# Attention scores in quarters of the TensorE array, and the opening's planner told so

## The chip, the cores and the metric

The kernel runs on one core of a Trainium2 chip. The metric is the device time of one execution in microseconds (us), as a median over runs. The core's engines are TensorE (PE, with its weight loads shown apart as PEld), VectorE (DVE), ScalarE (ACT) and GpSimd (POOL); SyncE (SP) issues the DMAs. Each engine works through its own list of instructions in program order and waits on semaphores for the others. PE writes into PSUM, which DVE and ACT empty.

## What is computed

A decayed causal attention over 4 batches, 8 heads, 576 positions and head size 64, and two gated feed-forward blocks after it. Cut to what matters:

```
scores = q @ k.T / sqrt(64)                       # per batch and head
ret    = scores * Dmat[head]                      # Dmat = gamma ** (i - j) for i >= j, else 0
x      = ret @ v                                  # 2304 tokens x 512
h = x @ w_in;  x = (h * cos(h)) @ w_out           # 512 -> 2048 -> 512
xn = x / rms(x) * rms_g
out = (silu(xn @ w_gate) * (xn @ w_val)) @ w_out2 # 512 -> 1536 -> 512
```

## The kernel before, in words

**The attention** is worked in chunks of 128 positions: per batch four full chunks and one short chunk of 64. Two batches are worked side by side, so the loop in `opening` (line 842 on) runs over ten pairs k = 0 to 9, with the short chunks at k = 4 and k = 9. Within a chunk the masked scores are computed directly; what comes from earlier chunks comes through a running state (sum of decayed key times value). For each chunk there are these steps:

- `scores` (line 338; its matmul is line 347): for each of the four pairs of heads, two matmuls. The contraction is over the head size, 64, so the even head of the pair takes the upper 64 rows of the array and the odd head the lower 64, each over all 128 columns (128 keys), with 128 moving columns (128 queries). The two run in row halves at the same time, and each of the two halves writes to its own PSUM bank. In a short chunk there are 64 keys, and a matmul already takes a quarter of the array.
- `masked` (L353, on DVE): multiplies a bank by the falling factors into SBUF, one bank at a time.
- `from_state` (L365): queries times state, 64 rows by 64 columns, in quarters of the array in the order (0,0), (1,1), (0,1), (1,0), eight matmuls a chunk.
- `sums_kv` (L379) and `values` (L395): column halves, 128 rows by 64 columns. ACT scales keys (`scale_keys`, L324) and copies the state (`copy_state`, L384).
- `result` (L405, on DVE): moves the output bank into `xall` with the gamma factor.

**The first feed-forward block** starts while the attention still runs. Its weights come in 64-bit words and are turned into float by `Block` (lines 163 to 200): ACT L144 and L154, DVE L148 (clamp), L151 (shift), L157 (high words), L160 (add), then ACT L191 and DVE L136 split them in a high and a low part. A unit is one tile of tokens by one weight block: `hidden` (L242 to L244, three matmuls per product) into a PSUM bank, then the gate: ACT L521, DVE L524 (remainder), ACT L527 (sine), DVE L530 (product, which frees the bank), ACT L534, DVE L136; three units later `out_t` multiplies by the output weights. `FIRST = 6` units use the first token tile, with weight blocks 0 to 5; the next 16 use the second tile and begin again at block 0. While the attention is open there are three general banks, named `g`, shared by scores, the late outputs and `hidden`.

**The order of the work** up to unit 21 comes from a planner. `opening` makes a `Task` for every step, with its engine, a guess of its duration, what it comes after, what buffers it takes and gives, a due time (`key`) and, on PE, a mode: "rows", "quarters", "columns" or "whole". `lay_out` (line 823) then picks task by task. A PE task whose mode differs from the last one's is taken to start `SWITCH` = 0.2 us later (0.3 for "whole"). On each engine, of the tasks that could start within `SLACK` = 0.05 us of the earliest, the one with the least due time is taken:

```
            if x.mode and x.mode != mode[0]:
                begin = max(begin, free[x.engine] + SWITCH + (0.1 if x.mode == "whole" else 0.0))
...
                begin, x = min(((b, x) for b, x in found if b <= first + SLACK), key=lambda bx: bx[1].key)
```

The picks give the program order on PE, DVE, ACT and SP. The planner's times only sort the tasks; on the chip every engine starts when its semaphores let it. Loads on SP are chained one behind another (`PLAN`); `keep_x`, which writes the split first tile to DRAM, is the one other SP task. After unit 21 the order is written out by hand, and the second feed-forward block follows.

The functions that the change touches, and what calls them:

Of the kernel before, what the change touches and what calls it, by code (L numbers as in the profile page):

```python
# [30 lines left out]
P = 128  # L31
B, H, S, D = 4, 8, 576, 64
# [55 lines left out]
def body(ctx: ExitStack, tc, xy, xr, w1, w2, rg, gq, gk, mask, out):  # L88
    nc = tc.nc
# [28 lines left out]
    def acc_tile(m):  # L118
        return (psp if m < KC else late["psh"]).tile([P, 512], F32, tag=f"acc{m}", name="acc")

    def ps_tile():
        if "psh" not in late:
            return psa.tile([P, 512], F32, tag="g", bufs=3, name="g")
        taken[0] += 1
        return hidden_tile() if taken[0] % 2 else acc_tile(KC + taken[0] // 2 % 2)
# [151 lines left out]
    def half(a):  # L277
        return slice(a * D, (a + 1) * D)
# [6 lines left out]
    def load(k, side, parts=(None,)):  # L285
        r, c = divmod(k, NCH)
        for part in parts:
            if len(ld.setdefault(k, [])) == side:
                x = wa.tile([P, 4, DM], F32, tag="w", name="x")
                ld[k].append(x)  # L290
            x = ld[k][side]
            if c == NFULL:
                nc.sync.dma_start(x.rearrange("p s m -> p (s m)"), xr[r])
            else:
                cols = slice(None) if part is None else slice(part * 2, part * 2 + 2)
                nc.sync.dma_start(x[:, cols], xy[r, c, side, :, cols])

    def keys_queries(n):
        b, c = chunks[n]
        k, q = b // 2 * NCH + c, b % 2  # L300
        if c < NFULL:
            parts = [ld[k][0][:, 2 * q + s] for s in range(2)]
        else:
            flat = ld[k][0].rearrange("p s m -> p (s m)")
            parts = [flat[:, (2 * q + s) * NPAIR * REST:(2 * q + s + 1) * NPAIR * REST] for s in range(2)]
        return [x.rearrange("p (a i) -> p a i", a=NPAIR) for x in parts]
# [13 lines left out]
    def scale_keys(k):  # L320
        kk, c = ld[k][1][:, 2:], k % NCH
        for h in range(H):
            x = kk[:, :, h * D:(h + 1) * D]
            nc.scalar.activation(x, x, AF.Copy, scale=decays[:, c * H + h:c * H + h + 1])  # L324
# [4 lines left out]
    def keys(w, a):  # L329
        return slice(None) if w == P else half(a)  # L330

    def spare_banks(n):
        b, c = chunks[n]
        return b % 2 and b // 2 * NCH + c < EARLY
# [5 lines left out]
    def scores(n):  # L340
        w = width(chunks[n][1])
        kt, qt = keys_queries(n)
        tiles = [acc_tile(2 + a) if spare_banks(n) else ps_tile() for a in range(2)]
        ps = raw_scores[n] = [tile.rearrange("p (h i) -> p h i", h=NPAIR) for tile in tiles]
        for p in range(NPAIR):
            for hh in range(2):
                nc.tensor.matmul(ps[hh][keys(w, hh), p, :w], kt[half(hh), p, :], qt[half(hh), p, :], start=True, stop=True)

    def masked(n, hh):
        w = width(chunks[n][1])  # L350
        s = sc[n, hh] = ap.tile([P, NPAIR, P], F32, tag=f"s{hh}", bufs=4, name=f"s{hh}")
        r = keys(w, hh)
        nc.vector.tensor_tensor(s[r, :, :w], raw_scores[n][hh][r, :, :w],  # L353
                                falling[hh if w == P else 2 * hh][r, :, :w], op=ALU.mult)

    def from_state(n):
        b, c = chunks[n]
        w, q, k = width(c), b % 2, b // 2 * NCH + c
        _, qt = keys_queries(n)
        if q == 0:  # L360
            begin_outputs(k)
        for j in range(2):
            for a, b in ((0, 0), (1, 1), (0, 1), (1, 0)):
                p, h = place(a, j, b)
                nc.tensor.matmul(outputs[k][a][half(b), q, j, :w], state[half(a), q, p, :], qt[half(a), p, :],  # L365
                                 start=q == 0 and j == 0, stop=False, skip_group_check=True)

    def sums_kv(n):
        b, c = chunks[n]
        q = b % 2  # L370
        vv, kk = tokens_of(n), ld[b // 2 * NCH + c][1][:, 2 + q]
        if c == 0 and q == 0:
            total[0] = psa.tile([P, 2, NPAIR, D], F32, tag="st", name="total")
        for j in range(2):
            for e in range(2):
                for a in range(2):
                    p, h = place(a, j, a ^ e)
                    cs = slice(h * D, (h + 1) * D)
                    nc.tensor.matmul(total[0][half(a), q, p, :], kk[:, cs], vv[:, cs], start=c == 0 and q == 0 and p == 0, stop=True,  # L379
                                     skip_group_check=True)  # L380

    def copy_state(k):
        for p in range(NPAIR):
            nc.scalar.activation(state[:, :, p, :], total[0][:, :, p, :], AF.Copy, scale=factors[:, k % NCH + 1, p:p + 1])  # L384
# [121 lines left out]
    def hidden(t, f):  # L506
        n = TILES[t][1]
        ps = ps_tile()
        proj(part1("in", f), t, ps)
        return ps[:, :n]  # L510
# [361 lines left out]
    def opening():  # L872
# [8 lines left out]
        def fetch(size, run, *take):  # L881
            queue.append(Task("SP", size, run, (), ones(*take), behind=queue[-1] if queue else None))
            return queue[-1]

        for k in PLAN:
            if k == 0:
                start = [fetch(0.0, load_first, "wa"), fetch(1.3, lambda: load(0, 0, range(1, 2)))]
# [12 lines left out]
        for k in range(B // 2 * NCH):  # L900
            b, c = k // NCH * 2, k % NCH
            full = c < NFULL
            pair = [(b + q) * NCH + c for q in range(2)]
            at = lead(k)
            bank = "acc" if k < EARLY else "g"
            places = {n: "more" if spare_banks(n) else "g" for n in pair}
            masks = {}
            for n in pair:
                score = Task("PE", 0.89 if full else 0.45, lambda n=n: scores(n), [start[0] if n == 0 else loads[k][0]], {places[n]: 2},
                             key=at - 2.0, more=0.25, mode="rows")  # L910
                masks[n] = [Task("DVE", 0.6 if full else 0.35, lambda n=n, hh=hh: masked(n, hh), [score, falls[hh if full else 2 * hh]],
                                 ones(f"s{hh}"), ones(places[n]), key=at - 2.0) for hh in range(2)]
            held = {bank: 1 if k < EARLY else 2}
            last = []
            if c > 0:
                for n in pair:
                    last = [Task("PE", 0.45 if full else 0.22, lambda n=n: from_state(n), masks[n] + before + last, held if n == pair[0] else (),
                                 ones("wa") if full and n == pair[1] else (), key=at, more=0.25, mode="quarters")]
                froms[k] = last
            adding = []  # L920
            if full:
                adding = [Task("ACT", 8 * 0.29, lambda k=k: scale_keys(k), [loads[k][1]], key=at - 1.0)]
                for n in pair:
                    adding = [Task("PE", 0.52, lambda n=n: sums_kv(n), before + adding + loads[k], ones("st") if c == 0 and n == pair[0] else (),
                                   key=at + 0.1, more=0.25, mode="columns")]
                before = [Task("ACT", 4 * 0.3, lambda k=k: copy_state(k), adding + last + froms.get(k - 1, []), (),
                               ones("st") if c == NFULL - 1 else (), key=at - 1.0)]
            for n in pair:
                after = masks[n] + last + loads[k] + (adding if n == pair[1] else [])
                give = {"s0": 1, "s1": 1, "wa": 0 if n == pair[0] else 2 if c == 0 else 1}  # L930
                last = [Task("PE", 0.79 if full else 0.42, lambda n=n: values(n), after, held if c == 0 and n == pair[0] else (), give,
                             key=at + 0.2, more=0.25, mode="columns")]
            freed = [{}, {bank: 1}] if k < EARLY else [{bank: 1}] * 2
            done = [Task("DVE", 0.6 if full else 0.35, lambda k=k, a=a: result(k, a), last + [gams], (), freed[a], key=at - 0.5) for a in range(2)]
            for n in pair:
                evacs[n] = done
        Task("ATT", 0.0, close_attention, [x for done in evacs.values() for x in done], (), {"g": 1, "wb": NSLOT_B})
        ready_w = {}
        for k in range(NW1):
            at = unit(first_use[k]) - LEAD  # L940
# [17 lines left out]
        for i in range(MANUAL):  # L958
            s, t, f = STEPS[i]
            at = unit(i)  # L960
            give = {f"x{kc}": 1 for kc in range(KC)} if i in ENDS else {}
            hiddens[i] = Task("PE", 2.72, lambda i=i: first_half(i), [ready_w[f], hiddens.get(i - 1)] + xs_of[s], ones("g"), give,
                              key=at, more=0.25, mode="whole")
# [35 lines left out]
    for i in range(MANUAL, LAST + LAG):  # L999
        early_out = LAG <= i < LAST and (i - LAG in ENDS or i == MANUAL)  # L1000
        if i < LAST:
# [3 lines left out]
            ps = hidden(t, f)  # L1005
# [360 lines left out]
```

## Time and profile before

| what | value |
|---|---|
| median of 3 runs | 869.49 us (868.59 to 870.76) |
| the profiled execution | 869.32 us |
| its span, first to last instruction | 867.5 us |
| mean granted TensorE clock | 0.998 |
| instructions | 13936, of them 5360 matmul records |

The profile is of one execution. Its span leaves out what lies before the first and after the last instruction. Times within it are us from the span's start. A matmul of f32 operands stands in it as two records, so that the 8 matmuls of one chunk's scores show as x16. The ends of matmuls are modelled, so the distance between two starts is the better measure of what a block of matmuls takes.

### The profile page before, as it was taken

The page shows a single profiled execution, that of the slowest core. Times are in us where ns is not written, and L with a number is a line of the kernel's source. Part 1 is how long each engine was busy: PE and PEld are TensorE (multiplying, and loading weights), DVE is VectorE, ACT ScalarE, POOL GpSimd, SP SyncE. Part 2 cuts the span into 40 slices and gives each one's busy share as a digit, 9 for nine tenths or more (in the row PEclk, how much of TensorE's full clock was granted, in tenths as well). Part 3 has the DMA queues.
Part 4 walks back from the last instruction along what each step waited for, and adds up shares of the span by engine and source line. Part 5 has one row for each costly group of instructions (what it writes and reads, how often), then busy time and mean ns, then how long its engine had stood idle before and what let it go on. Part 6 is the DMA issues. An engine that isn't in the chain of part 4 may idle for free.

```text
span 867.5 us, 13936 instructions
## 1 busy us (share of the span) xinstructions
PE 852.7 (98%) x5360; PEld 780.0 (90%) x5360; DVE 655.7 (76%) x998; ACT 487.3 (56%) x885; POOL 65.7 (8%) x77
## 2 busy tenths in 40 slices
PE   6999999999999999999999999999999999999998
PEld 5887788888888889988889999999999999999998
DVE  3899999857879976997875888898565598343594
ACT  5789786457655566675566565554443353333351
POOL 0000000000000000002443544000000000000000
PEclk9999999999999999999999999999999999999999
DMA  8999401044434443334785888998777797877792
GB/s 344 416 417 414 183 17 48 2 133 154 138 110 145 147 146 102 117 122 154 253 286 219 312 317 321 342 315 267 282 254 245 221 299 273 282 252 253 211 313 101
DMA packets 58530, 193.68 MB, mean 223 GB/s; under 512 B 5472, under 2 KB 20960, under 8 KB 49760
## 3 DMA queue, kind: packets, MB, share of 16 engines
q1 hardware_dynamic: 58464, 192.80, 64.1%
q8 instruction: 42, 0.69, 0.3%
q14 instruction: 24, 0.20, 0.1%
HBM read 143.49 MB, written 49.28 MB: 222 GB/s over the span
## 4 chain that ended last, share of the span: by engine, by line
PE 81%; DMA 9%; DVE 8%; ACT 1%; issue 1%; SPq 0%; ACTq 0%; DVEq 0%
PE h L1104 15%; PE acc L1104 14%; PE acc L243 10%; PE acc L244 10%; PE acc L242 10%; PE acc L1151 10%; DMA x<-xy_dram 6%; PE h L243 3%; PE h L244 3%; PE h L242 3%; DVE SV L1140 3%; DVE w L136 2%; DMA kept_x<-xhi 2%; DMA rg_sb<-rg_dram 1%; ACT w L1132 0%
## 5 line engine op out<-in xcount | busy, mean ns | idle before, releaser
L1104 PE MATMUL acc<-w 128*128 128x384 f32 x720 | 139.3, 335 | 0.2
L1104 PE MATMUL h<-w 128*128 128x384 f32 x720 | 138.8, 335 | 0.5 <-DVE SV L1086 0.5
L1104 PEld LDWEIGHTS h<-w 128*128 128x128 f32 x720 | 125.9, 188 | 1.5 <-DVE SV L1086 0.8
L1104 PEld LDWEIGHTS acc<-w 128*128 128x128 f32 x720 | 126.0, 188 | 0.9 <-DVE v L1092 0.8
L243 PE MATMUL acc<-glo,w 128*128 128x512 f32 (+1 forms) x320 | 117.9, 368 | 0.0
L242 PE MATMUL acc<-ghi,w 128*128 128x512 f32 (+1 forms) x320 | 117.9, 368 | 0.0
L244 PE MATMUL acc<-ghi,w 128*128 128x512 f32 (+1 forms) x320 | 117.7, 368 | 0.0
L1151 PE MATMUL acc<-w 128*128 128x384 f32 x564 | 100.8, 335 | 1.0 <-DVE w L136 1.0
L658 POOL TENSOR_TENSOR z<-z 128x256 f32<-128x256 f32 x72 | 65.3, 909 | 477.8 <-DMA z<-w 416.9
L1151 PEld LDWEIGHTS acc<-w 128*128 128x128 f32 x564 | 98.0, 188 | 1.6 <-DVE w L136 1.6
L1092 DVE TENSOR_TENSOR v<-s,acc 128x384 f32<-128x384 f32 x54 | 29.9, 553 | 52.9 <-PE acc L1104 41.6
L243 PEld LDWEIGHTS acc<-glo,w 128*128 128x128 f32 x320 | 60.3, 188 | 10.5 <-DVE glo L136 0.4
L242 PEld LDWEIGHTS acc<-ghi,w 128*128 128x128 f32 x320 | 60.3, 189 | 10.1
L244 PEld LDWEIGHTS acc<-ghi,w 128*128 128x128 f32 x320 | 60.4, 189 | 9.8
L1132 ACT CAST w<-SV 128x768 fp32r<-128x768 f32 x55 | 42.5, 832 | 33.5 <-DVE SV L1140 18.5
L527 ACT ACTIVATE r<-r,half_pi 128x512 f32<-128x512 f32 (+1 forms) x80 | 54.7, 684 | 11.3 <-DVE r L524 10.8
L1086 DVE TENSOR_TENSOR SV<-s,h 128x384 f32<-128x384 f32 x54 | 29.8, 552 | 41.2 <-PE h L1104 35.6
L534 ACT CAST ghi<-r 128x512 fp32r<-128x512 f32 (+1 forms) x80 | 46.2, 577 | 20.8 <-DVE r L530 20.7
L1070 ACT COPY s<-h 128x384 f32<-128x384 f32 x54 | 25.8, 478 | 55.8 <-PE h L1104 54.4
L136 DVE TENSOR_TENSOR glo<-r,ghi 128x512 fp32r<-128x512 f32 (+1 forms) x80 | 52.2, 653 | 4.2 <-ACT ghi L534 3.2
L136 DVE TENSOR_TENSOR w<-SV,w 128x768 fp32r<-128x768 f32 x55 | 50.5, 962 | 5.6 <-ACT w L1132 5.6
L242 PE MATMUL h<-xhi,w 128*128 128x512 f32 (+1 forms) x148 | 54.2, 366 | 0.0
(130 smaller groups left out, 1596.8 us busy)
## 6 DMA issues: line engine op xcount, KB each, us to landing
w<-so SPq DMA_DIRECT2D x42, 768.0 KB, 5.6
w<-s SPq DMA_DIRECT2D x24, 1024.0 KB, 5.0
raw<-w_dram SPq DMA_DIRECT2D x36, 512.0 KB, 4.0
w<-s SPq DMA_DIRECT2D x24, 768.0 KB, 4.3
raw<-w_dram SPq DMA_DIRECT2D x16, 1024.0 KB, 15.0
x<-xy_dram SPq DMA_DIRECT2D x14, 1024.0 KB, 19.9
s<-w SPq DMA_DIRECT2D x12, 1024.0 KB, 6.2
w<-t SPq DMA_DIRECT2D x36, 256.0 KB, 2.3
```

The lines of the kernel that those rows point to most:

```text
L136: eng.tensor_tensor(dst, src, hi.bitcast(F32), op=ALU.subtract)
L242: nc.tensor.matmul(dst, a[0], b[0], start=start, stop=False)
L243: nc.tensor.matmul(dst, a[0], b[1], start=False, stop=False)
L244: nc.tensor.matmul(dst, a[1], b[0], start=False, stop=stop)
L527: nc.scalar.activation(s["r"], s["r"], AF.Sin, bias=half_pi, scale=1.0)
L534: nc.scalar.copy(s["hi"], s["r"])
L658: nc.gpsimd.tensor_tensor(z[:, dst], z[:, a], z[:, b], op=op)
L1086: nc.vector.tensor_tensor(dst, s, bank, op=ALU.add)
L1092: nc.vector.tensor_tensor(t, s, bank, op=ALU.add)
L1104: nc.tensor.matmul(bank, w[:, wp, kc * P:(kc + 1) * P], x[:, kc], start=k in (0, 1, 3) and kc == 0 and m == 0, stop=kc == 1 and m == 2, sk ...
L1132: nc.scalar.copy(t[:, 0], src)
L1151: nc.tensor.matmul(pair[d][:, :HALF], wi[:, a], s[:, b, i % 2], start=start and i == 0 and p == 0, stop=i == NPR - 1 and p == 2, skip_grou ...
```

## The change

In a full chunk each score matmul of 64 rows by 128 keys is cut in two of 64 rows by 64 keys. The four matmuls of a pair of heads take the four quarters of the array, in the order (0,0), (1,1), (0,1), (1,0), where the first number is the head's row half and the second the half of the keys; they write the same places of the same two banks. Short chunks keep their two matmuls per pair, written out so that they compute what they did. The planner's mode for a score task becomes "quarters", also for the short chunks; the task's guessed duration and due time stay.

```diff
         for p in range(NPAIR):
-            for hh in range(2):
-                nc.tensor.matmul(ps[hh][keys(w, hh), p, :w], kt[half(hh), p, :], qt[half(hh), p, :], start=True, stop=True)
+            for hh, m in ((0, 0), (1, 1), (0, 1), (1, 0)) if w == P else ((0, 0), (1, 1)):
+                nc.tensor.matmul(ps[hh][half(m), p, :w], kt[half(hh), p, m * D:(m + 1) * D] if w == P else kt[half(hh), p, :],
+                                 qt[half(hh), p, :], start=True, stop=True)
...
                 score = Task("PE", 0.89 if full else 0.45, lambda n=n: scores(n), [start[0] if n == 0 else loads[k][0]], {places[n]: 2},
-                             key=at - 2.0, more=0.25, mode="rows")
+                             key=at - 2.0, more=0.25, mode="quarters")
```

## Rows read from the trace of the kernel before

**Rows 1.** The page: busy time, share of the span, instructions of each engine.
```profile
PE 852.7 (98%) x5360; PEld 780.0 (90%) x5360; DVE 655.7 (76%) x998; ACT 487.3 (56%) x885; POOL 65.7 (8%) x77
```

**Rows 2.** Busy us by stretch: start:end, length, engines (instructions), clock, DMA share, GB/s.
```profile
19.40:31.45 12.05, 12.04 (x224) 11.45 (x226) 6.35 (x10) 7.37 (x25) 0.00 (x0) 0.87 1.01 419
31.45:41.00 9.55, 9.10 (x229) 8.08 (x225) 9.32 (x14) 5.61 (x13) 0.00 (x0) 1.00 1.01 411
41.00:69.00 28.00, 27.99 (x420) 23.57 (x420) 27.90 (x43) 25.34 (x58) 0.00 (x0) 1.00 1.01 415
69.00:99.50 30.50, 28.56 (x261) 22.39 (x256) 30.21 (x42) 26.00 (x36) 0.00 (x0) 1.00 0.65 264
...
110.00:440.00 330.00, 330.00 (x1637) 280.76 (x1636) 275.46 (x460) 207.39 (x355) 18.38 (x20) 1.00 0.39 121
```

**Rows 3.** Waits, 30 to 100 us: who <- whom: us in total, times, longest.
```profile
DVE xall L405 <- PE po L395: 2.1, 1, 2.1
PE g L242 <- DVE r L530: 2.0, 4, 0.8
...
PE po L365 <- DVE xall L405: 0.4, 2, 0.2
```

**Rows 4.** Timeline of PE, 15 to 30 us: start, us, line, out<-in, shapes, records.
```profile
15.34 1.10 PE L365 MATMUL po<-x,state 64*64 64x128 f32 x32
19.41 2.08 PE L347 MATMUL g<-x 64*128 64x128 f32 x16 [2.97 <-DMA x<-xy_dram]
21.29 1.66 PE L347 MATMUL acc<-x 64*128 64x128 f32 x16
22.87 1.15 PE L379 MATMUL total<-x 128*64 128x64 f32 x32
...
25.70 1.16 PE L347 MATMUL g<-x 64*128 64x128 f32 x16
...
27.69 1.10 PE L365 MATMUL po<-x,state 64*64 64x128 f32 x32
28.72 1.15 PE L379 MATMUL total<-x 128*64 128x64 f32 x32
```

**Rows 5.** Timeline of PE, blocks of one chunk alone, with what follows each.
```profile
46.39 1.10 PE L365 MATMUL po<-x,state 64*64 64x128 f32 x16
...
48.51 0.67 PE L365 MATMUL po<-x,state 64*64 64x128 f32 x16
49.10 1.97 PE L395 MATMUL po<-s,x 128*64 128x128 f32 x32
...
60.10 1.16 PE L347 MATMUL g<-x 64*128 64x128 f32 x16
61.19 0.50 PE L242 MATMUL g<-xhi,w 128*128 128x512 f32 x1
```

**Rows 6.** Timeline of DVE: the wait at 31.45, weight block 6, the last product.
```profile
31.45 1.29 DVE L405 TENSOR_TENSOR xall<-po,gam 128x512 f32<-128x512 f32 x2 [2.07 <-PE po L395]
...
87.92 0.69 DVE L148 TENSOR_SCALAR t<-t 128x1024 f32<-128x1024 f32 x1
...
91.77 0.68 DVE L151 TENSOR_SCALAR t<-t 128x1024 int32<-128x1024 int32 x1
...
93.88 1.22 DVE L157 SCALAR_TENSOR_TENSOR t<-raw,t 128x1024 int32<-128x1024 int32 x1
95.13 1.23 DVE L160 CUSTOM_DVE_ANT_0 t<-raw,t 128x2048 uint16<-128x2048 uint16 x1
...
98.79 0.69 DVE L530 TENSOR_TENSOR r<-g,r 128x512 f32<-128x512 f32 x1
```

**Rows 7.** Timeline of PE, 99 us: the first matmul of unit 6, its idle time before.
```profile
99.53 0.51 PE L242 MATMUL g<-xhi,w 128*128 128x512 f32 x1 [0.77 <-DVE r L530]
```

**Rows 8.** Busy us by stretch around the load that lands at 19.41, columns as in Rows 2.
```profile
19.00:21.00 2.00, 1.58 (x14) 1.59 (x16) 0.00 (x0) 0.00 (x0) 0.00 (x0) 0.53 1.00 414
...
23.00:26.00 3.00, 3.00 (x68) 2.83 (x70) 1.66 (x3) 2.34 (x9) 0.00 (x0) 1.00 1.00 410
```

## The prediction

> **What bounds the kernel now.** I read the busy line of the page first. The reader is to see that TensorE (PE) is busy in 98% of the span [rows 1]: time falls only where PE loses work or an idle gap. The scores belong to the opening, so next I cut that into stretches. From 19.40 to 31.45 PE is busy 12.04 of 12.05 us while VectorE (DVE) works 6.35. From 41 to 69 both are full (27.99 and 27.90 of 28.00). From 69 to 99.5 DVE is full (30.21 of 30.50) and PE has 1.94 us of gaps; from 110 to 440 PE has none [rows 2]. The waits name the gaps: four times the projection (L242) waits for the product L530, which frees its PSUM bank, 2.0 us together, and twice `from_state` waits for an evacuation, 0.4 us. DVE for its part has one wait worth a row between 30 and 100 us, 2.1 us for the `values` matmuls of L395; it ends at 31.45 [rows 3, 6]. So the chain changes hands: a load that lands at 19.41, PE until 31.45, DVE's list until 99.53, where PE begins unit 6 [rows 4, 6, 7], then PE to the end. What PE saves before 31.45 brings DVE's list forward; what it saves between 31.45 and 99.5 mostly makes the L530 gaps longer; and by then all scores are done.
>
> **The matmuls.** There are 16 full chunks (k = 0 to 3 and 5 to 8, two batches each); the four short chunks already use quarters and keep their two matmuls per head pair, so only their planner mode changes. A full chunk goes from 8 matmuls to 16. The trace records each f32 matmul twice, so its 16 records become 32, and PE's count becomes 5360 + 16 x 16 = 5616.
>
> In row halves two chunks take 25.70 to 27.69 = 1.99 us [rows 4] and one alone takes 60.10 to 61.19 = 1.09 [rows 5]: a chunk is worth 0.90 and the change of array mode 0.19. The kernel's own quarter matmuls, `from_state` at L365 with 64x64 weights and 128 moving columns, show the other price: two chunks in 27.69 to 28.72 = 1.03 [rows 4], one alone in 48.51 to 49.10 = 0.59 [rows 5], so 0.44 per 8 matmuls and 0.15 for the mode. Twice 0.44 is 0.88 against 0.90. The same work runs twice as often, each piece on half the columns, four pieces at a time instead of two. I take 0.88: the same shapes in the same order of quarters. The upper bound is 1.80, if the two quarters of one row half did not overlap; unlike L365 they read the same moving rows at once, and no row shows that. Weight loads are hidden beside the matmuls in both forms. So the matmuls alone give 16 x 0.02 = 0.3 us on PE, of which four chunks (k = 2 and 3, between 19.41 and 27.69) lie on the chain: 4 x 0.02 = 0.1 us.
>
> **The mode change.** Between a score block and a neighbouring `from_state` block the array now stays in quarters. That removes 0.15 to 0.19 us per border. Three such borders show: at 15.34, where PE afterwards waits for the load until 19.41 [rows 4], so it is worth nothing; at 27.69, on the chain, worth 0.17 (the middle); and at 46.39, in the stretch where DVE is full [rows 2, 5], worth nothing. The Trainium skill (TensorEngine Tiling (Array Packing), Tiling Modes, Key Properties) says that changing the tiling mode, not just the tile, drains TensorE. It names no time; the 0.15 to 0.19 us agree with it.
>
> **The planner.** Telling it "quarters" takes its 0.2 us off the start of a score task behind `from_state` and the reverse. It picks the next task by start, and by due time within 0.05 us, so tasks change places: on PE a `from_state` may now come between two score tasks; on DVE and ScalarE the masks and state copies that follow them move against weight splitting and the gate's products. SP's loads stay in their chained order, though `keep_x` may be issued past another raw load; it doesn't wait there for the score. POOL has no planned task. In each score block the first mask still waits for nearly the whole block, since a bank's last quarter is the last or last but one matmul. So the masks are no earlier, and they queue behind whatever DVE is doing. The order's effect isn't in the trace of before; I bound it. Gain: the DVE steps that PE doesn't need by 99.53 are four of weight block 6 (L148, L151, L157, L160; first used six units later): 0.69 + 0.68 + 1.22 + 1.23 = 3.8 us [rows 6]. But PE can gain no more than its gaps, 2.0 + 0.4 = 2.4 us [rows 3]. Loss: another such set of four, 3.8 us, ahead of the last product. The likeliest is near zero, since the old order already fills PE and DVE to 99% from 41 to 69: I take 0.
>
> **Sum.** 0.1 + 0.17 is 0.3 us. DVE starts its continuous run at about 31.15 and PE unit 6 at about 99.2. Against the profiled execution that is 869.32 - 0.3 = 869.0; that execution has 1.8 us outside its span of 867.5 and lies 0.17 us under the median, so against the median 869.49 it is **869.2 us**.
>
> **Rivals.** A measurement of this kernel can tell about 0.3%, 2.6 us, from no change: faster means under 866.9, slower over 872.1.
>
> *The new order fills the gaps (faster).* Block 6's steps go behind the last product, and PE runs through from 31.45. For it: 3.8 us of steps could wait. Against: PE must lose all of its 2.4 us of gaps to get to 869.2 - 2.4 = 866.8, barely past the bound. The clock could help: PE idles from 16.4 to 19.41 and then runs at a granted 0.53 (its 1.2 GHz level), and is back at 1.00 (2.4 GHz) in 23 to 26 [rows 8]; the two blocks of 19.41 took 22.87 - 19.41 = 3.46 us instead of 1.99 [rows 4], 1.5 us that a run without the fall would not pay. But nothing in the change shortens the wait for the load, so I expect it again.
>
> *The new order puts work ahead of the last product (slower).* PE begins unit 6 when the L530 of 98.79 frees the bank [rows 6, 7]; DVE has no slack there, so every step planned in front moves it. Four more steps cost 3.8 us: 869.2 + 3.8 = 873.0. It decides for slower from 2.9 us of added steps on. For it: one task list, sorted anew. Against: the due times of weight block 7 lie later than the product's, and only a start earlier by over 0.05 us overrides them.
>
> *The added matmuls cost a start of their own (slower).* If a chunk takes e more, the four on the chain give 4e, and the eight of k = 5 to 8 give 8e less the 2.4 us of gaps. At the upper bound e = 0.90 that is 3.6 + 4.8 = 8.4 us, 877.6; from e = 0.44 on (12e - 2.4 = 2.9) it is over the bound. L365's 0.44 for 16 records speaks against any e. The Trainium skill (TensorEngine Tiling (Array Packing), Instruction Overhead) gives each matmul about 60 cycles on trn2 and advises against taking the tiling factor from a dimension that is already small: an estimate of 25 ns at 2.4 GHz, 0.4 us for 16 more records, which would make 869.2 + 1.6 + 0.8 = 871.6. The 0.44 us for 16 quarter records, 27 ns apart, include any such overhead.
>
> *Nothing moves.* If the planner's order stays and DVE hides the 0.3 us too, it is 869.5, the same verdict.
>
> **The numbers.** The forecast with "nothing moves" has 0.72, the filled gaps 0.13, the steps ahead of the product 0.11, the added starts 0.04: faster 0.13, same 0.72, slower 0.15. The range reaches down past 866.8 to 866.4, since gaps and clock could come together in part, and up to the bound of slower, 872.2; it leaves out the two slower cases, 0.15, and little of the faster one.
>
> **What would show it.** Right: 32 score records per chunk about 27 ns apart, two chunks in about 1.9 us; the DVE evacuation of 31.45 some 0.3 us earlier; the same four product gaps of about 2 us; unit 6 at 99 to 99.5. Wrong: score chunks over 1.3 us; DVE idle between masks after 31; unit 6 before 97 or after 102; more weight steps ahead of the last L530; PE gaps after 110.

## The result: slower, and the profile after

The changed kernel takes 873.36 us (median of 11 runs) against 869.79 us for the kernel before in the same comparison: a ratio of 1.0051, 95% interval 1.0038 to 1.0063. That is slower by more than the 0.3% that counts, and outside the predicted range of 866.4 to 872.2. The profiled execution took 874.0 us, 4.7 us more than that of before; its span is 872.2 us.

First the page of the changed kernel: the busy line, and the lines on its DMA queues.

```profile
PE 852.0 (98%) x5616; PEld 779.2 (89%) x5616; DVE 656.1 (75%) x998; ACT 487.8 (56%) x885; POOL 64.8 (7%) x77
...
q1 hardware_dynamic: 58464, 192.80, 63.8%
q8 instruction: 44, 0.72, 0.3%
```

The 5616 records are as predicted, and PE is busy for 0.7 us less than before [rows 1]. So PE has no more work; it has more idle time. The last line looks harmless, and it is where the time went: 44 packets of an instruction queue, 0.72 MB, which is 16 KB each. PE has 2 x 5616 = 11232 weight loads and matmuls, and 11232 / 44 is about 255 instructions per packet. The page of before has 42 packets there, two fewer for its 512 fewer instructions:

```profile
q8 instruction: 42, 0.69, 0.3%
```

The stretches of the changed kernel, in the columns of [rows 2]:

```profile
19.40:31.45 12.05, 10.27 (x280) 9.37 (x274) 6.24 (x10) 7.30 (x25) 0.00 (x0) 1.00 1.01 414
31.45:41.00 9.55, 7.72 (x214) 7.08 (x211) 9.12 (x14) 5.54 (x13) 0.00 (x0) 1.00 1.01 414
41.00:69.00 28.00, 24.88 (x491) 21.49 (x491) 23.48 (x36) 21.45 (x54) 0.00 (x0) 0.94 1.01 416
```

PE is idle for 1.8 us in the first, 1.8 in the second and 3.1 in the third, where it had 0, 0.4 and 0. DVE, full from 41 to 69 before (27.90 of 28.00), now does 23.48 there. It waits for PE's `values` blocks, as at 31.45 before, but more often, and once for a score block. Its waits from 41 to 69 us, where before it has none (who, for whom, us in total, times, longest):

```profile
DVE xall L406 <- PE po L396: 3.2, 2, 2.5
DVE s L354 <- PE acc L347: 1.1, 1, 1.1
```

All waits from 0 to 115 us, in the same form:

```profile
DVE xall L406 <- PE po L396: 8.4, 4, 3.8
...
PE po L366 <- issue: 2.4, 2, 1.4
PE po L396 <- issue: 2.2, 1, 2.2
...
PE total L380 <- issue: 1.7, 1, 1.7
...
PE acc L347 <- issue: 1.3, 1, 1.3
```

"Issue" is a wait for nothing that the profile shows: the semaphores were there and the engine did not go on. Before, PE's matmuls have no such wait from 30 to 100 us. The timeline of PE shows where these fall; the last number of a row is its count of matmul records:

```profile
26.84 0.80 PE L380 MATMUL total<-x 128*64 128x64 f32 x18
29.33 0.62 PE L380 MATMUL total<-x 128*64 128x64 f32 x14 [1.70 <-issue]
29.74 1.97 PE L396 MATMUL po<-s,x 128*64 128x128 f32 x32
31.49 1.15 PE L380 MATMUL total<-x 128*64 128x64 f32 x32
32.57 1.29 PE L366 MATMUL po<-x,state 64*64 64x128 f32 x29
33.60 0.27 PE L347 MATMUL g<-x 64*64 64x64 f32 x2
33.69 0.28 PE L366 MATMUL po<-x,state 64*64 64x128 f32 x3
33.71 0.53 PE L347 MATMUL g<-x 64*64 64x64 f32 x11
34.08 0.22 PE L347 MATMUL acc<-x 64*64 64x64 f32 x1
34.08 0.22 PE L347 MATMUL g<-x 64*64 64x64 f32 x1
34.14 0.22 PE L347 MATMUL acc<-x 64*64 64x64 f32 x1
34.14 0.28 PE L347 MATMUL g<-x 64*64 64x64 f32 x2
35.74 0.67 PE L347 MATMUL acc<-x 64*64 64x64 f32 x14 [1.32 <-issue]
```

The gap at 29.33 is in the middle of a block of one kind, and so is the one at 35.74: nothing in the program is special there. But from one to the next there are 14 + 32 + 32 + 29 + 2 + 3 + 11 + 1 + 1 + 1 + 2 = 128 records, each with its weight load: 256 instructions. The next two gaps, at 41.92 and 47.99, come after 127 and 128 records more. I call these places marks. Setting the marks against the packets of the instruction queue (from the trace's DMA records, in us from the span's start) gives the table below. "Reaches" and "goes on" are the starts of the matmul records before and behind a mark, and the last column counts from "goes on":

```
              PE reaches  goes on  gap    the block's fetch   next fetch starts after
before   3      34.13      34.37   0.24     31.81-32.83          3.66
before   4      40.36      40.52   0.16     38.03-39.05          3.59
before   5      47.23      47.42   0.20     44.11-45.18          3.08
changed  1      15.73      16.97   1.24     14.36-15.36          3.62
changed  2      22.80      23.15   0.36     20.59-21.61          3.61
changed  3      27.42      29.33   1.92     26.76-27.84          3.82
changed  4      34.20      35.74   1.54     33.15-34.29          3.61
changed  5      40.27      41.92   1.65     39.35-40.41          3.64
changed  6      45.51      47.98   2.47     45.57-46.67          3.77
changed  7      54.01      54.20   0.20     51.75-52.85          3.58
```

At each mark of the changed kernel PE goes on 1.3 to 1.6 us after the block's 16 KB have moved. The next fetch starts 3.6 to 3.8 us after PE goes on, and a packet takes 1.0 to 1.1 us. So while PE starves, one block of 256 instructions costs 3.7 + 1.05 + 1.45 = 6.2 us, however fast PE works. Between its marks 3, 4, 5 and 6 PE needed only 4.87, 4.53 and 3.59 us. The kernel before crosses the same places with at most 0.24 us lost. At its marks 3 and 4 it too goes on 1.5 us after the block has moved: it was already at the edge, and its spare was spent by 16 more records per chunk. At its mark 5 the block has been there for 2.24 us; the 0.20 us there is the step from L365 to L379, a change of array mode.

### The profile page after: what moved, and what is told of

Read it like the earlier page. It is cut to its first block, busy times and chain, and to the rows that moved or that the text cites. A ratio compares the mean times of both kernels' runs of the same rounds, so it can differ in the third digit from the quotient of the medians.

```text
span 872.2 us, 14455 instructions
## 1 busy us (share of the span) xinstructions
PE 852.0 (98%) x5616; PEld 779.2 (89%) x5616; DVE 656.1 (75%) x998; ACT 487.8 (56%) x885; POOL 64.8 (7%) x77
## 4 chain that ended last, share of the span: by engine, by line
PE 84%; DVE 9%; DMA 3%; issue 2%; ACT 1%; SPq 1%; POOL 0%; DVEq 0%; ACTq 0%; POOLq 0%
PE acc L1105 15%; PE h L1105 15%; PE acc L243 10%; PE acc L242 10%; PE acc L244 10%; PE acc L1152 10%; PE h L242 3%; PE h L244 3%; PE h L243 3%; DVE SV L1141 3%; DVE w L136 3%; DMA kept_x<-xhi 2%; DMA x<-xy_dram 2%; PE po L396 1%; PE total L380 1%
```

## The experiments

Theory 1: PE's instruction stream runs dry. Its rivals: theory 2, the planner's new order, and theory 3, something in the score quarters themselves. Each run is compared with the kernel before on the same chip.

**Quarter matmuls, old plan** (the changed kernel with one word put back):

```diff
-                             key=at - 2.0, more=0.25, mode="quarters")
+                             key=at - 2.0, more=0.25, mode="rows")
```

> Quarter matmuls with the planner's mode left at rows, so that PE, DVE and ACT work in the order of before. Theory 1 (PE's instruction stream runs dry: it comes in blocks of 16 KB, 256 instructions, and a chunk of quarter scores has 64 of them where row halves have 32): slower by 3 to 5 us, as the changed kernel; gaps of 1.2 to 2.5 us without a releaser before every 128th matmul record between 16 and 50 us, 6 to 10 us together. Theory 2 (the planner's new order makes it slower): within 1 us of before, and no such gaps.

Measured: 873.36 us against 869.00, ratio 1.0048 (1.0034 to 1.0062). PE's waits in its timeline:

```profile
16.72 0.66 PE L366 MATMUL po<-x,state 64*64 64x128 f32 x13 [0.90 <-issue]
36.75 0.68 PE L347 MATMUL acc<-x 64*64 64x64 f32 x14 [1.04 <-issue]
42.94 0.40 PE L366 MATMUL po<-x,state 64*64 64x64 f32 x12 [1.44 <-issue]
49.00 1.96 PE L396 MATMUL po<-s,x 128*64 128x128 f32 x15 [2.20 <-issue]
```

With the order of before on PE, DVE and ACT the loss is all there, and so are the gaps (5.6 us in these rows; fewer than expected, since at the second and third mark little is lost). The order is not needed for it.

Part of the loss goes with PE's clock, which falls to its lower level after some of PE's idle times (in the changed kernel it is granted at 0.57 from 48 to 52 us, behind the gap at 47.99). The three executions of this run with a granted clock of 0.998 took 871.88 to 872.62 us, against 867.74 to 869.87 for the kernel before at the same 0.998: some 3 us at the same clock. The other three, at 0.994 to 0.996, took 874.10 to 874.18.

**Row-half matmuls, new plan** (the kernel before with the other word):

```diff
-                             key=at - 2.0, more=0.25, mode="rows")
+                             key=at - 2.0, more=0.25, mode="quarters")
```

> Row-half matmuls with the planner's mode at quarters: the changed kernel's order with the old matmuls. Theory 1 (instruction stream): within 1 us of before, gaps without a releaser under 0.5 us each. Theory 2 (order): slower by 3 to 5 us.

Measured: 868.91 us against 869.00, ratio 1.0002 (0.9992 to 1.0012). No matmul waits for "issue" here; a weight load does for 0.6 us at most. The waits from 12 to 104 us:

```profile
PEld g L347 <- issue: 1.4, 6, 0.4
PEld po L365 <- issue: 1.0, 2, 0.6
```

Theory 2 falls. The new order does change PE's gaps before the projection (0.8 us in two, where before had 2.0 in four [rows 3]), but the time stays.

**Quarters in k = 0 to 3 alone, and in k = 5 to 8 alone**, both with the old plan; in `scores`:

```diff
+            k = chunks[n][0] // 2 * NCH + chunks[n][1]
+            if w == P and not (k < 4):        # the other run: k > 4
+                for hh in range(2):
+                    nc.tensor.matmul(ps[hh][:, p, :w], kt[half(hh), p, :], qt[half(hh), p, :], start=True, stop=True)
+                continue
```

The lines of the change follow, for the other chunks.

> Quarters in the eight full chunks of k = 0 to 3 alone, planner's mode rows: 256 more PE instructions before about 27 us, one block. Theory 1: about half of the loss, 1.5 to 3 us; the first gaps without a releaser stand as in the changed kernel up to 36 us (about 5 us together), smaller after. Theory 2: within 1 us of before.

> Quarters in the eight full chunks of k = 5 to 8 alone, planner's mode rows. Theory 1: gaps only after 36 us, where before already crosses its blocks with 0.2 us to spare or less: 1 to 2.5 us slower. Theory 2: within 1 us of before.

Measured: 869.79 us for the first four, ratio 1.0010 (1.0001 to 1.0018), and 872.71 us for the last four, 1.0036 (1.0023 to 1.0049). The first four cost less than the 1.5 to 3 us expected, and the last four, 3.7 us, more than the 1 to 2.5. The first have gaps (1.07 at 17.02, 1.05 at 37.01, 0.77 at 43.24), but the one at 17.02 lies ahead of a load that PE waits for anyway, and after 43 it catches up with the edge. The last four have one large gap, 2.21 us at 48.12, and most of the loss. I read this as: what a gap costs depends on who waits behind it, and at 48 us that is DVE, full there in the kernel before. The clock has a part too: behind that gap it is granted at 0.66 from 48 to 52 us. And the last four spread widely: two of their 12 executions, both with a granted clock of 1.000, took 868.92 and 869.15 us, hardly more than the kernel before, and the other ten, at 0.994 to 0.998, took 871.0 to 874.6. Only one of the twelve has a trace, so whether those two had the gap at 48 us stays open.

**The number of instructions without the quarters.** The kernel before, with every `values` matmul of a full chunk cut in two over its queries:

```diff
-                nc.tensor.matmul(outputs[k][a][half(b), q, j, :w], vv[keys(w, a), h * D:(h + 1) * D], sc[n, a][keys(w, a), p, :w],
-                                 start=c == 0 and q == 0 and j == 0, stop=True, skip_group_check=True)
+                for i in range(0, w, 64):
+                    nc.tensor.matmul(outputs[k][a][half(b), q, j, i:i + 64], vv[keys(w, a), h * D:(h + 1) * D], sc[n, a][keys(w, a), p, i:i + 64],
+                                     start=c == 0 and q == 0 and j == 0 and i == 0, stop=True, skip_group_check=True)
```

> The kernel before, scores in row halves and its order unchanged, but every values matmul of a full chunk is cut in two over its 128 queries: 16 records more per chunk, as many as the change adds to the scores, with the same columns streamed in all. Theory 1 (number of PE instructions): slower by 3 to 5 us, with gaps of 1 to 2.5 us without a releaser before every 128th matmul record between 16 and 50 us. Theory 3 (something about the score quarters themselves, such as their weight loads): within 1.5 us of before and no such gaps.

Measured: 876.28 us against 869.29, ratio 1.0081 (1.0062 to 1.0099). Its PE waits:

```profile
31.24 0.51 PE L396 MATMUL po<-s,x 128*64 128x64 f32 x11 [0.34 <-issue]
37.26 1.62 PE L396 MATMUL po<-s,x 128*64 128x64 f32 x46 [1.45 <-issue]
43.67 0.46 PE L396 MATMUL po<-s,x 64*64 64x64 f32 x15 [1.92 <-issue]
50.24 1.16 PE L347 MATMUL acc<-x 64*128 64x128 f32 x15 [1.72 <-issue]
57.46 0.73 PE L396 MATMUL po<-s,x 128*64 128x64 f32 x16 [2.18 <-issue]
```

The scores are in row halves, the order is that of before, and the gaps come all the same, 6.0 to 7.2 us apart. Theory 3 falls: it is the count. It costs more than the 3 to 5 us expected, and more than the change. Two things can add to it, and no run separates them. Four of its gaps, 1.4 to 2.2 us, stand between 37 and 57 us, on the path to DVE. And the cut matmuls aren't quite free by themselves: a `values` block of two chunks takes 2.02 us here (46.13 to 48.15), where before has 1.85 (43.45 to 45.30).

**Why is a fetch so slow?** Theory A: its packet queues behind the loads, which keep the DMA engines full (a share of 1.01 in the stretches above). Theory B: it takes that long in any case. A first pair thinned the weight loads to 1 KB of 8 per partition, with zeros from GpSimd in the rest, once in the kernel before and once in the changed one:

```diff
-            eng.dma_start(self.raw.rearrange("p n c w -> p (n c w)"), src.bitcast(I32))
+            flat = self.raw.rearrange("p n c w -> p (n c w)")
+            nc.gpsimd.memset(flat[:, 256:].bitcast(F32), 0.0)
+            eng.dma_start(flat[:, :256], src.bitcast(I32)[:, :256])
```

> The kernel before, but each load of a block of the first weights moves 1 KB of its 8 KB per partition, and GpSimd fills the rest with zeros, so that the product with most of these weights is left out. It is the pair's other half to the next run: after the attention's own loads are in, the DMA engines are no longer full. Both theories: no gap without a releaser over 0.5 us; time within 3 us of before, since VectorE's work is unchanged.

> The changed kernel with the same thin weight loads and the same part left out. Theory A (a block of PE instructions is late because its fetch queues behind the loads on full DMA engines): where the engines are not full, the 3.6 to 3.8 us between crossing a mark and the start of the fetch shrink below 2.5 us, the gaps without a releaser after 40 us go, and the run is within 1.5 us of the thin row halves. Theory B (the fetch takes as long however busy the engines are): 3.6 to 3.8 us everywhere PE is starved, gaps of 1.2 to 2.5 us as in the changed kernel, 3 to 5 us slower than the thin row halves.

Measured: 873.86 us for row halves, ratio 1.0050 (1.0033 to 1.0068), and 878.99 us for quarters, 1.0105 (1.0086 to 1.0124). The gaps stayed (2.48 us at 47.80), and the difference of 5.1 us is what theory B expected or a little more. But the pair does not decide, since the loads that were left kept the engines full until about 54 us, past the gaps, and there theory A expects the same. The row halves also missed their own expectation of 3 us, which is told in the last section. So a second pair thinned the attention's loads of k = 5 to 8 to a quarter as well:

```diff
+                if k > NFULL:
+                    nc.gpsimd.memset(x[:, 1:], 0.0)
+                    cols = slice(0, 1)
                 nc.sync.dma_start(x[:, cols], xy[r, c, side, :, cols])
```

> As the thin row halves, and in addition every attention load of k = 5 to 8 moves one quarter of its bytes, with zeros in the rest: those chunks are left out of the result, but their instructions all run. The loads should be done by about 40 us, so that the DMA engines are idle while PE still works on k = 5 to 8. Both theories: no gap without a releaser over 0.5 us.

> The same in the changed kernel, with the same parts left out. Theory A (the fetch of a block of PE instructions queues behind the loads): gaps without a releaser as before at the first four marks, up to about 36 us, while the engines are full; then the wait from a mark to the start of the next fetch falls from 3.6 to 3.8 us to under 2.5 us, and the gaps of 1.6 and 2.5 us that stand at 40 to 48 us in the changed kernel shrink to under 0.5 us. Time within 2.5 us of the run with few loads in row halves. Theory B (the fetch takes as long however busy the engines are): the gaps at 40 to 48 us stay at 1.2 to 2.5 us with 3.6 to 3.8 us to the start of each fetch; slower than its row halves by 3 to 5 us.

Measured: 873.19 us for row halves, ratio 1.0053 (1.0034 to 1.0073), and 874.31 us for quarters, 1.0069 (1.0051 to 1.0087). The difference of quarters to row halves is 1.1 us, where it was 5.1 in the pair before. Two stretches of the quarters with few loads, in the columns of [rows 2], and its PE waits from 12 to 60 us:

```profile
40.00:44.00 4.00, 3.40 (x130) 2.99 (x132) 4.00 (x8) 4.00 (x12) 2.48 (x2) 1.00 0.57 222
44.00:48.00 4.00, 3.89 (x84) 3.12 (x82) 4.00 (x8) 4.00 (x14) 1.59 (x1) 1.00 0.92 304
```

```profile
16.48 0.66 PE L371 MATMUL po<-x,state 64*64 64x128 f32 x13 [0.80 <-issue]
29.35 0.62 PE L385 MATMUL total<-x 128*64 128x64 f32 x14 [0.56 <-issue]
34.66 0.67 PE L352 MATMUL acc<-x 64*64 64x64 f32 x14 [0.23 <-issue]
```

The same two stretches of the changed kernel:

```profile
40.00:44.00 4.00, 2.56 (x115) 2.31 (x109) 3.24 (x6) 3.98 (x11) 0.00 (x0) 1.00 1.01 414
44.00:48.00 4.00, 1.80 (x47) 1.56 (x43) 2.63 (x5) 3.09 (x12) 0.00 (x0) 1.00 1.00 410
```

With the DMA share at 0.57 and 0.92 instead of 1.00, PE's gaps for instructions are gone and DVE is full, though the zero fills may be slowing it too (last section). The marks of the run with few loads:

```
              PE reaches  goes on  gap    the block's fetch   next fetch starts after
quarters 1      15.42      16.48   1.07     13.99-14.97          3.59
quarters 3      28.57      29.35   0.78     26.90-27.97          2.72
quarters 4      34.21      34.66   0.44     32.07-33.21          1.21
quarters 5      40.36      40.36   0.00     35.86-36.79          1.45
quarters 6      44.64      44.65   0.00     41.81-42.82          1.56
quarters 7      49.80      49.80   0.00     46.21-47.35          0.53
```

Marks 5 to 7, without a gap, prove nothing by their last column. Where nothing starves PE, a fetch can begin earlier than the array shows: in the kernel before, the fetch that comes in order behind the mark at 174.28 starts at 169.45. And with full engines the kernel before crosses a mark freely at 56.09 and has its next fetch 0.95 us later. What can be compared are marks at which PE starved. After every gap over 1 us in the runs with full engines the next fetch starts about 3.5 us later or more. At mark 4 here PE starved too (it goes on 1.45 us after its block has moved), and the next fetch starts after 1.21 us. The stretches from going on to that fetch, in the columns of [rows 2], at mark 4 of the changed kernel, at mark 4 of this run, and at 56.09 of the kernel before:

```profile
35.74:39.35 3.61, 3.61 (x86) 3.37 (x90) 3.33 (x6) 0.83 (x1) 0.00 (x0) 1.00 1.05 431
34.66:35.86 1.20, 1.20 (x25) 1.13 (x26) 1.20 (x2) 0.33 (x2) 1.20 (x1) 1.00 0.44 145
56.09:57.04 0.95, 0.95 (x32) 0.78 (x30) 0.95 (x2) 0.95 (x2) 0.00 (x0) 1.00 1.04 431
```

The first two are the same place in the same list of instructions, with a DMA share of 1.05 and of 0.44. So 3.6 us is not a fixed delay, which is theory B. Nor does the fetch wait until PE has come to a fixed place in its block, a rival not listed above: PE was 86 records past the mark in one and 25 in the other. The transfer itself stays at about 1.0 us, and the gaps at the early marks, expected as in the changed kernel, are smaller too. Theory A holds in this: how late the fetch of a block of PE instructions starts depends on the loads. One starved mark shows it directly, and the gaps that go agree. Where the fetch waits, in a queue of the DMA engines or ahead of it, no run shows.

No run points to a version that beats the kernel before: the quarters win nothing that shows once they are fed (1.1 us slower with few loads, where DVE is full), and before loses at most 0.6 us at its listed marks.

## Why the prediction was wrong

**The step that failed** is the part on the matmuls. It counted 256 more records, priced them by PE's time alone, 0.88 us a chunk, and put the instructions that carry them at nothing, without a reason. In its place the runs show that a block of 256 instructions costs 6.2 us while the DMA engines are full, and PE gaps of 8.1 us at marks 2 to 7 above. The price it took was right: in the changed kernel two chunks of scores take 24.06 to 25.86 = 1.80 us with no mode change behind them.

```profile
24.06 1.10 PE L347 MATMUL g<-x 64*64 64x128 f32 x32
24.99 1.05 PE L347 MATMUL acc<-x 64*64 64x128 f32 x32
25.86 1.05 PE L366 MATMUL po<-x,state 64*64 64x128 f32 x32
```

That is 0.19 us less than the 1.99 of [rows 4]; the prediction had 0.21, 0.17 for the mode and 0.04 for the matmuls. But blocks of 16 and 32 records, which it read the price from, are shorter than a block of 128, so they cannot show what a steady stream costs. What could have been read before: the page's 42 packets of the instruction queue, 16 KB or 256 instructions each; the small "issue" waits in front of weight loads; and, at marks 3 and 4, that PE goes on just 1.5 us after its block has moved, where mark 5 has 2.24. The distance of the packets, 6.1 to 6.4 us from 25 to 50 us, could not by itself tell a floor from PE's own pace. But it would have made a late block of instructions a rival with a price.

**The chain** was read rightly, and it says how the gaps become time. DVE's list waits for PE's `values` blocks: the evacuation that started at 31.45 starts at 31.53 instead of the predicted 31.15, after a wait of 3.82 us, and it waits 2.46 us once more at 49.09. Between 41 and 69 us DVE waits 4.3 us where before it had no wait. Unit 6 begins at 103.93 instead of 99.53 [rows 7], 4.4 us late, and the span ends 4.7 us late:

```profile
31.53 1.29 DVE L406 TENSOR_TENSOR xall<-po,gam 128x512 f32<-128x512 f32 x2 [3.82 <-PE po L396]
...
49.09 1.29 DVE L406 TENSOR_TENSOR xall<-po,gam 128x512 f32<-128x512 f32 x2 [2.46 <-PE po L396]
```

```profile
103.93 0.50 PE L242 MATMUL g<-xhi,w 128*128 128x512 f32 x1 [0.18 <-DVE r L531]
```

The gaps at marks 2 to 7 are 8.1 us where the listed marks of before have 0.6. Not all of that arrives. In this execution the load for k = 2 let PE start at 18.92 instead of 19.41, and its clock did not fall there (1.00 from 19 to 21), so that its first two blocks took 1.91 us instead of 3.46 [rows 4, 8]: 2.0 us back. I don't count it to the change: the run with the new plan alone waits longer for that load, 3.31 us, and keeps a clock of 1.00 there as well. After the gap at 48 us the clock fell instead: in the stretch from 48 to 52 it is granted at 0.57, and the score block of 49.41 took 1.76 us, where that of 24.06 took 0.93. The prediction had the clock as a possible gain alone.

Of its own signs of being wrong two came, DVE idle after 31 us and unit 6 after 102. The score chunks stayed under 1.3 us, as it held.

**The planner** was put at 0 with bounds of 2.4 us of gain and 3.8 of loss: right, since the new order alone measures 1.0002. The mode change fits in size: with the matmuls' 0.04 it makes 0.21 us, and 0.19 came.

**The rivals.** Steps put ahead of the last product: not so, since the new order alone costs nothing; that its 873.0 lies next to the measured 873.36 is luck. The added matmuls cost a start of their own: the sign was right and the cause not. That rival had the same e for every chunk, and L365's 27 ns per record was rightly held against it; the loss is not per matmul but per 256 instructions, and only where the fetch is slow. So its chance of 0.04 was too small, as it was the one case in which more instructions cost anything at all.

The Trainium skill (Runtime: NRT & Kernel Launch, Instruction fetch mechanics) says that an engine's instructions are refilled in blocks of 16 KiB, 256 instructions, by a DMA queue of the sequencer's own, and that crossing a boundary is mostly hidden. The traces agree on the block: 16 KB packets, and gaps 128 records apart. They disagree on the hiding where the DMA engines are full and PE's matmuls are small: 1.2 to 2.5 us at five of the seven marks of the changed kernel. Here the measurement decides.

## What to carry to other kernels

Count PE's instructions, not only its time: a matmul cut in pieces of the same total streaming time is free only while the stream of 256-instruction blocks keeps pace. Compare the time PE takes for 128 f32 matmul records with the time in which a block of instructions came here while loads kept the DMA engines full, 6.2 us; where PE needs less, every added instruction is on the path. The distance between packets alone says nothing: from 170 to 230 us of the kernel before they are 28 to 30 us apart because PE takes that long for 256 instructions of larger matmuls, and none of its marks there is late. A wait for "issue" in the middle of a block of one kind, repeated at a fixed count of instructions, is the sign, and the first thing to ask is what keeps the fetch waiting.

## What was not expected of the hardware

- One late block of instructions costs PE up to 2.5 us, and how late its fetch starts depends on the other traffic: 3.5 us or more after a starved mark with the DMA engines full, 1.2 us after one at a share of 0.44.
- The fetch is only one block ahead while PE starves: at marks 2 to 7 of the changed kernel a block's packet starts after PE went on at the mark before it.
- GpSimd's zero fills slowed DVE in the runs with thin loads. L151 of DVE takes 0.69 us by itself; beside a fill it took 2.04, and over the seven of the first 100 us its mean rose from 689 to 1076 ns, that of L148 from 683 to 834. That is 3.8 us on a full DVE and would account for most of the 4.6 us that the thin row halves lost; no run has the thin loads without the fills. From the timelines of DVE and of POOL in that run:

```profile
62.23 2.04 DVE L151 TENSOR_SCALAR t<-t 128x1024 int32<-128x1024 int32 x1
```

```profile
62.06 1.67 POOL L169 MEMSET raw<- 128x1792 f32 x1 [1.60 <-issue]
```
